# Two more turns of u given to the DMA crossbar, and another search over the order of instructions

## The chip, the cores and the metric

One core of one Trainium2 chip. The metric is the device time of one execution in microseconds (us); the profile's span is some 2 us shorter than the time of the same execution. Each kernel was run several times (an execution over 1.5% above the fastest of its kernel counts as slow).

## The reference

Attention with a block-causal mask over 8 batches, then a mixer over tokens and over channels:

```
scores = q @ k.T / 8                    # 8 batches, 8 heads, 576 tokens, 64 wide
attn   = softmax(where(block_i >= block_j, scores, -1e9))      # blocks of 64 tokens
x  = (attn @ v) as [batch, 576, 512]
h  = relu(x.T @ w_tok1) @ w_tok2        # over tokens, 576 -> 256 -> 576
u  = x + h.T
h2 = relu(u @ w_ch1) @ w_ch2            # over channels, 512 -> 1536 -> 512
out = u + h2                            # float32
```

## The kernel before

The kernel keeps everything in bfloat16 on the chip. Its parts are operations in a planner, which knows a cost for each, simulates the engines with a list schedule, perturbs priorities at random, keeps what ends earlier, and emits the instructions in the order found. The order is therefore fixed before the run, and a wait that the planner did not foresee stalls an engine on the spot (9.9 us of TensorE in the changed kernel).

The up projection over channels needs u transposed (`uT`, channels on partitions), the residual at the end needs u itself. Three ways occur:

```python
# batch 0: uT is made directly; at the down projection TensorE turns it back into the same bank
for m in range(NDM) if turned and part == 0 else ():
    nc.tensor.matmul(out=ps[:, 128*m : 128*(m+1)], lhsT=uT[b % 2][:, si, m, :], rhs=ident,
                     start=(m == 0), stop=False)
# batch 1: u is made, and TensorE transposes it (4 chunks, and one of leftover rows, umt)
for m in range(NDM):
    nc.tensor.transpose(ps[:, 128*m : 128*(m+1)], src[:, 128*m : 128*(m+1)], ident)
# batches 2 to 7: the DMA crossbar transposes it, 256 KB at a time, issued from SP
nc.sync.dma_start_transpose(out=uT[b % 2][:, 2*f : 2*f+2]..., in_=ut[:, 2*f : 2*f+2, :]...)
```

All loads of q, k, v and of the weights after the first are issued by GpSimd and cast float32 to bfloat16 on the way. q and k have a ring of three buffers, v of two, so batch b's loads run while earlier batches compute. The down projection's weights come in three parts:

```python
for c in range(0, NDC, 4):
    nc.gpsimd.dma_start(out=wc2_sb[:, c : c + 4, :],
        in_=moe_w_ch2[128*c : 128*(c+4), :].rearrange("(p c) t -> p c t", c=4))
```

How the planner counts transfers: it has one clock for GpSimd's queue (`soft`) and one for SP's and ScalarE's (`hard`). A load is counted after earlier transfers of SP, but a transfer of SP is never delayed by loads:

```python
if e == "POOL": soft = max(soft, hard, first) + o.xfer
else:           hard = max(hard, first) + o.xfer
```

The softmax here doesn't subtract the row's maximum and nothing guards it: scores larger than these inputs give would overflow.

Of the kernel before, what the change touches and what calls it, by code (L numbers as in the profile page):

```python
# [30 lines left out]
class Plan:  # L31
# [37 lines left out]
    def search(self, tries):  # L69

        prios = [o.prio for o in self.ops]
        modes = [o.mode for o in self.ops]
        slots = {name: list(free) for name, free in self.free.items()}

        def run(prios):
            for o, prio, mode in zip(self.ops, prios, modes):
                o.prio, o.mode = prio, mode
            self.free = {name: list(free) for name, free in slots.items()}
            try:
                order = self.run()  # L80
            except ValueError:
                return math.inf, ()
            return max(o.end for o in order if not o.quick), order

        rnd = random.Random(0)
        movable = [n for n, prio in enumerate(prios) if abs(prio) < 4e3]
        best = run(prios)[0]
        for _ in range(tries):
            moved = list(prios)
            count, width = rnd.choice((1, 2, 4, 8, 30, 100)), rnd.choice((0.3, 1, 3, 10))  # L90
            for n in rnd.sample(movable, count):
                moved[n] += rnd.uniform(-width, width)
            end = run(moved)[0]
            if end <= best:
                best, prios = end, moved
        return run(prios)[1]
# [98 lines left out]
def kernel(  # L195
# [71 lines left out]
    def bank_of(note):  # L267
        return mm[note["slot"]]
# [486 lines left out]

    def first_uT(x_done, a_done, w2_ready):

        xt, at = x_sb[0], aT[0]
        done = []
        for m in range(NDM):  # L760
            bank = {}

            def emit(o, m=m, bank=bank):
                for c in range(4):
                    nc.tensor.matmul(  # L765
                        out=bank_of(bank)[:, 128 * c : 128 * c + 128],
                        lhsT=xt[:, c, 128 * m : 128 * (m + 1)],
                        rhs=ident,
                        start=(c == 0),
                        stop=False,  # L770
                    )

            first = P.add(
                "PE", mm_cost(128, 4), emit, x_done[2 * m : 2 * m + 2] + pads["ident"], -2700 + m,
                take=[(BANK, bank)], urgent=1,
            )

            def emit(o, m=m, bank=bank):
                for t in range(NDT):
                    nc.tensor.matmul(  # L780
                        out=bank_of(bank),
                        lhsT=at[:, t, 128 * m : 128 * (m + 1)],
                        rhs=w2_sb[:, t, 0:512],
                        start=False,
                        stop=(t == NDT - 1),
                    )

            op = P.add("PE", mm_cost(512, 2), emit, [a_done[m], first] + w2_ready, -2700 + m, urgent=1)
            reads(("a", 0), op)
            reads(("x", 0), op)  # L790

            def emit(o, m=m, bank=bank):
                ps = bank_of(bank).rearrange("p (c s) -> p c s", c=4)
                if o.engine == "ACT":
                    nc.scalar.copy(uT[0][:, :, m, :], ps)
                else:
                    nc.vector.tensor_copy(uT[0][:, :, m, :], ps)

            done.append(P.add(EVAC, evac_cost(512), emit, [op], -2700 + m, give=[bank], urgent=1))
        return done  # L800

    def token_mix(b, x_done, w1_ready, w2_ready):
# [10 lines left out]
        if b == 0:  # L813
            a_all = [
                token_up(0, slice(128 * m, 128 * m + 128), (0, 1), x_done[2 * m : 2 * m + 2], [], w1_ready, -2800 + m, 1)
                for m in range(NDM)
            ]
            done = first_uT(x_done, a_all, w2_ready)
            prio = 0.5
        else:  # L820
            a_all = [
                token_up(b, slice(0, DM), (tt,), x_done, a_war, w1_ready, prio) for tt in range(NDT)
            ]
        for si in range(4 if b == 0 else 0, 4):
            bank = {}

            def emit(o, si=si, bank=bank):
# [54 lines left out]
                reads(("x", (b - 1 + i) % 3), um_rows[-1])  # L882


        crossbar = b >= 2
        for f in range(2 if crossbar else 0):
            def emit(o, f=f):
                nc.sync.dma_start_transpose(
                    out=uT[b % 2][:, 2 * f : 2 * f + 2].rearrange("p c m s -> p (c m) s"),
# [3 lines left out]
            op = P.add("SP", 2.0, emit, u_done[2 * f : 2 * f + 2] + uT_war, prio, xfer=3.0)  # L893
            reads(("u", b % 3), op)
            done.append(op)
        if crossbar and odd:
            def emit(o):
                nc.sync.dma_start_transpose(out=umT[pair % 2], in_=umt)

            op = P.add("SP", 1.0, emit, um_rows + reuse(("umT", pair % 2)), prio, xfer=1.0)  # L900
            reads(("um", pair % 2), op)
            um_done.append(op)
        for si in () if crossbar or b == 0 else range(4 + odd):
            bank = {}

            def emit(o, si=si, bank=bank):
                ps = bank_of(bank).bitcast(BF16)[:, 0:512]
                src = ut[:, si, :] if si < 4 else umt
                for m in range(NDM):
                    nc.tensor.transpose(  # L910
                        ps[:, 128 * m : 128 * (m + 1)], src[:, 128 * m : 128 * (m + 1)], ident
                    )

            deps = ([u_done[si]] if si < 4 else um_rows) + pads["ident"]
            deps += uT_war if si < 4 else reuse(("umT", pair % 2))
            op = P.add(
                "PE", mm_cost(128, 4), emit, deps, prio + 2 + 0.1 * si, take=[(BANK, bank)]
            )
            reads(("u", b % 3) if si < 4 else ("um", pair % 2), op)

            def emit(o, si=si, bank=bank):
                ps = bank_of(bank).bitcast(BF16)[:, 0:512].rearrange("p (m s) -> p m s", m=NDM)
                dst = uT[b % 2][:, si] if si < 4 else umT[pair % 2]
                if o.engine == "ACT":
                    nc.scalar.copy(dst, ps)
                else:
                    nc.vector.tensor_copy(dst, ps)

            op = P.add(
                EVAC, {"ACT": act_cost(512), "DVE": dve_cost(512, 2)}, emit, [op], prio, give=[bank]  # L930
            )
            (done if si < 4 else um_done).append(op)
        return done, um_done, u_done, um_rows

    a_even = {}
# [61 lines left out]
    def channel_down(b, g_done, wc2_ready, u_done, prio, mixed=False):  # L997
        chunks = [None] if mixed else list(range(4))
        gt = gmT[b // 2 % 2] if mixed else gT[b % 2]
        ut = um_sb[b // 2 % 2] if mixed else u_sb[b % 3]  # L1000

        turned = b == 0 and not mixed
        prev = None
        for n, si in enumerate(chunks):
            c0 = 0 if mixed else 128 * si
# [8 lines left out]
            for cols in (slice(0, 256), slice(256, 512)) if last else (slice(0, 512),):  # L1014
# [4 lines left out]
                for part in range(3):  # L1019
                    def emit(o, part=part, si=si, c0=c0, cols=cols, width=width, bank=bank):  # L1020
                        ps = bank_of(bank)[:, 0:width]
                        for m in range(NDM) if turned and part == 0 else ():
                            nc.tensor.matmul(  # L1023
                                out=ps[:, 128 * m : 128 * (m + 1)],
                                lhsT=uT[b % 2][:, si, m, :],
                                rhs=ident,
                                start=(m == 0),
                                stop=False,
                            )
                        for cc in range(4 * part, 4 * part + 4):  # L1030
                            nc.tensor.matmul(  # L1031
                                out=ps,
                                lhsT=gt[:, cc, c0 : c0 + 128],
                                rhs=wc2_sb[:, cc, cols],
                                start=(cc == 0 and not turned),
                                stop=(cc == NDC - 1),
                            )


                    gs = g_done[part : part + 1] if mixed else g_done[4 * part : 4 * part + 4]  # L1040
                    deps = [prev] + gs + wc2_ready[part : part + 1] + (u_done if part == 0 else [])
                    cost = mm_cost(width, 4) + (mm_cost(128, 4) if turned and part == 0 else 0)
                    prev = P.add(
                        "PE", cost, emit, deps, prio + 0.1 * n - 0.01 * part + cols.start * 1e-4,
                        take=[(BANK, bank)] if part == 0 else (),
                    )
                reads(("gm", b // 2 % 2) if mixed else ("g", b % 2), prev)
                if turned:
                    reads(("uT", b % 2), prev)

                def emit(o, si=si, oi=oi, n=n, cols=cols, width=width, bank=bank):
                    dst, ps = o_sb[oi][:, n % 2, cols], bank_of(bank)[:, 0:width]
                    if turned:
                        cast(o, dst, ps)
                    else:
                        nc.vector.tensor_tensor(  # L1056
                            out=dst, in0=ps, in1=(ut if mixed else ut[:, si, :])[:, cols], op=ADD
                        )

                op = P.add(  # L1060
                    EVAC if turned else "DVE", evac_cost(width), emit, [prev] + u_done + o_war, prio, give=[bank]
                )
                reads(("um", b // 2 % 2) if mixed else ("u", b % 3), op)
                halves.append(op)
# [55 lines left out]
                channel_down(p, g_done, wc2_ready, u_done, 10 * p + 4)  # L1120

    with tc.manual_schedule():
        for op in P.search(1000):
            op.emit(op)


# [28 lines left out]
```

## Time and profile before

| | kernel before |
|---|---|
| time, median | 306.5 us (306.05 to 306.92) |
| span of the profile | 304.3 us |
| TensorE busy | 98% |
| DMA before 68 us | about 200 GB/s; the load queue's packets take 130% of the 16 engines' time |
| crossbar transposes | 12 to `uT`, 3 to `umT`, all from 84.8 us on, land in 2.4 to 4.9 us |

A share over 100%, as this 130%, means that several packets are open on an engine at once. The lines themselves are in the prediction.

### The profile page before, as it was taken

To read this page: it belongs to the slowest core of one execution; us is meant where nothing else is said; L and a number is where in the kernel's file an instruction comes from. 1 tells how busy PE (TensorE), PEld (TensorE's weight loads), DVE (VectorE), ACT (ScalarE), POOL (GpSimd) and SP (SyncE) were. 2 spreads that over 40 slices of the span, in tenths; PEclk is the share of its full clock that TensorE was granted. 3 is DMA by queue.
4 is the path that set the end of the run, shared out by engine and by line. 5 is a ranking of instruction groups with operands and counts; after the bars stand their busy time and mean duration, and the time that the engine had idled before them with its cause. 6 is when DMAs were issued, how large, how long until landed. Compare 5 with 4: busy or idle time off the path is not lost.

```text
span 304.3 us, 7056 instructions
## 1 busy us (share of the span) xinstructions
PE 296.9 (98%) x2999; PEld 160.7 (53%) x3034; DVE 155.5 (51%) x380; ACT 164.6 (54%) x233; POOL 62.1 (20%) x96
## 2 busy tenths in 40 slices
PE   8999999999999999999999999999999999999995
PEld 4575456465454564555554564645446545555443
DVE  5566539989595599584987253615023021010112
ACT  5887855677855756875557856324413503615300
POOL 9766454702610602600140000000000000000000
PEclk9999999999999999999999999999999999999999
DMA  8999999995982998975193002033113222100133
GB/s 202 179 196 209 200 191 187 220 216 91 142 121 44 161 119 139 189 46 60 54 107 88 2 2 53 18 95 97 36 32 140 46 80 49 43 26 2 69 138 106
DMA packets 64383, 31.94 MB, mean 105 GB/s; under 512 B 53088, under 2 KB 55008, under 8 KB 64352
## 3 DMA queue, kind: packets, MB, share of 16 engines
q0 software_dynamic: 44320, 17.34, 48.9%
q1 hardware_dynamic: 19744, 13.57, 17.1%
q10 hardware_dynamic: 288, 0.59, 0.5%
q8 instruction: 23, 0.38, 0.5%
q14 instruction: 8, 0.07, 0.1%
HBM read 35.85 MB, written 9.44 MB: 149 GB/s over the span
## 4 chain that ended last, share of the span: by engine, by line
PE 95%; DMA 2%; issue 1%; DVE 1%; ACT 0%; ACTq 0%
PE mm L1031 31%; PE mm L947 28%; PE mm L555 10%; PE sc L508 10%; PE mm L736 6%; PE mm L829 4%; PE mm L974 4%; DMA gT<-in_q_dram 2%; PE mm L860 1%; PE mm L332 1%; PE mm L780 0%; PE mm L910 0%; DVE qT L393 0%; PE mm L1023 0%; PE mm L765 0%
## 5 line engine op out<-in xcount | busy, mean ns | idle before, releaser
L527 ACT ACTIVATE e_sb<-sc 128x1024 bf16<-128x1024 f32 x95 | 92.5, 1028 | 26.3 <-PE sc L508 24.5
L947 PE MATMUL mm<-uT,wc_sb 128*128 128x512 bf16 x384 | 91.2, 380 | 0.1
L1031 PE MATMUL mm<-wc_sb,gT 128*128 128x512 bf16 (+1 forms) x372 | 89.4, 372 | 1.5 <-issue 0.5
L722 ACT ACTIVATE gT<-mm 128x512 bf16<-128x512 f32 x74 | 44.2, 597 | 63.1 <-PE mm L947 62.8
L947 PEld LDWEIGHTS <-wc_sb 128*128 128x128 bf16 x384 | 41.9, 114 | 39.3 <-issue 3.9
L1031 PEld LDWEIGHTS <-gT 128*128 128x128 bf16 x396 | 36.9, 98 | 40.8 <-issue 3.3
L1056 DVE TENSOR_TENSOR o_sb<-mm,u_sb 128x512 f32<-128x512 f32 (+1 forms) x29 | 19.5, 672 | 74.5 <-PE mm L1031 74.3
L422 POOL DMA_DIRECT2D v<-in_v_dram x45 | 37.2, 839 | 35.3 <-PE sc L508 23.6
L508 PE MATMUL sc<-qT,kT 32*128 32x64 bf16 (+4 forms) x744 | 35.4, 281 | 0.5 <-DVE qT L393 0.5
L555 PEld LDWEIGHTS <-e_sb 128*128 128x128 bf16 x896 | 31.1, 97 | 8.0 <-issue 3.6
L555 PE MATMUL mm<-v,e_sb 128*128 128x65 bf16 x896 | 33.9, 193 | 0.1
L583 DVE TENSOR_TENSOR x_sb<-mm,rinv 128x320 bf16<-128x320 f32 x64 | 31.0, 491 | 2.0
L724 DVE TENSOR_SCALAR gT<-mm 128x512 bf16<-128x512 f32 x22 | 15.2, 689 | 15.9 <-PE mm L947 15.7
L844 DVE TENSOR_TENSOR u_sb<-mm,x_sb 128x512 bf16<-128x512 f32 x28 | 18.0, 686 | 10.2 <-PE mm L829 9.0
L393 DVE STREAM_TRANSPOSE qT<-qraw 128x288 int32<-128x288 int32 x32 | 21.6, 706 | 3.0 <-PE sc L508 2.1
L393 DVE STREAM_TRANSPOSE kT<-kraw 128x288 int32<-128x288 int32 x32 | 20.9, 703 | 4.3 <-DMA kraw<-in_k_dram 1.7
L508 PEld LDWEIGHTS <-kT 32*128 32x128 bf16 x752 | 12.3, 93 | 19.8 <-issue 16.7
L736 PE MATMUL mm<-x_sb,w_sb 128*128 128x512 bf16 (+1 forms) x98 | 18.0, 314 | 0.3
L533 DVE MEMSET e_sb<- 64x128 uint32 (+1 forms) x72 | 10.5, 153 | 14.7 <-ACT e_sb L527 11.4
L373 POOL DMA_DIRECT2D qraw<-in_q_dram x15 | 8.3, 552 | 42.2 <-DVE qT L393 28.5
L577 DVE RECIPROCAL rinv<-mm 128x5 f32<-128x5 f32 x64 | 11.4, 185 | 7.4 <-PE mm L555 6.7
L722 ACT ACTIVATE aT<-mm 128x512 bf16<-128x512 f32 (+1 forms) x15 | 8.1, 543 | 12.3 <-PE mm L736 12.3
(66 smaller groups left out, 175.6 us busy)
## 6 DMA issues: line engine op xcount, KB each, us to landing
out_dram<-o_sb SPq DMA_DIRECT2D x15, 512.0 KB, 2.9
kraw<-in_k_dram POOLq DMA_DIRECT2D x15, 288.0 KB, 7.7
qraw<-in_q_dram POOLq DMA_DIRECT2D x15, 288.0 KB, 7.2
v<-in_v_dram POOLq DMA_DIRECT2D x28, 128.0 KB, 6.9
wc_sb<-in_moe_w_ch_dram POOLq DMA_DIRECT2D x8, 192.0 KB, 7.1
wc_sb<-in_moe_w_ch_dram POOLq DMA_DIRECT2D x3, 512.0 KB, 10.4
out_dram<-o_sb SPq DMA_DIRECT2D x10, 128.0 KB, 2.3
v<-in_v_dram POOLq DMA_DIRECT2D x15, 64.0 KB, 6.1
```

The source lines that it names most:

```text
L393: nc.vector.transpose(dst[:, 0:S, :] .rearrange("p s e -> p (s e)") .bitcast(I32) .rearrange("p (a k) -> p k a", k=NB)[:, k0:k1], raw2.bit ...
L422: nc.gpsimd.dma_start(out=dst, in_=src)
L508: nc.tensor.matmul(out=home(n)[:, c0 : c0 + w], lhsT=kT[i][r, j0 : j0 + 128, par], rhs=qT[i][r, i0 : i0 + w, par], start=(par == 0), stop= ...
L527: nc.scalar.activation(dst, sc[SC.index(note["pool"])][:, :, 0:n], EXP, scale=scale)
L555: nc.tensor.matmul(out=u[:, I, 0:65], lhsT=w, rhs=vt[:, J, head, 0:65], start=(J == 0), stop=(J == I),)
L583: nc.vector.tensor_tensor(out=xt[:, :, 64 * head : 64 * head + 64], in0=u[:, :, 0:64], in1=ri.to_broadcast([128, 5, 64]), op=MULT,)
L722: nc.scalar.activation(dst, src, RELU)
L736: nc.tensor.matmul(out=bank_of(bank)[:, w * n : w * n + w], lhsT=wt[:, tt : tt + 255 : 2], rhs=xt[:, c, cols], start=(c == 0), stop=(c == 4),)
L844: nc.vector.tensor_tensor(out=ut[:, si, :], in0=bank_of(bank), in1=xt[:, si, :], op=ADD)
L947: nc.tensor.matmul(out=bank_of(bank), lhsT=wc1_sb[:, m, channels(cc)], rhs=uT[b % 2][:, :, m, :], start=(m == 0), stop=(m == NDM - 1),)
L1031: nc.tensor.matmul(out=ps, lhsT=gt[:, cc, c0 : c0 + 128], rhs=wc2_sb[:, cc, cols], start=(cc == 0 and not turned), stop=(cc == NDC - 1),)
L1056: nc.vector.tensor_tensor(out=dst, in0=ps, in1=(ut if mixed else ut[:, si, :])[:, cols], op=ADD)
```

## The change

The intent is to take 36 matmuls of 128 columns from TensorE, the engine that bounds the kernel (98% busy, 95% of the chain that ended last). Batch 0's u now comes from two crossbar transposes of `uT`, and batch 1's `uT` and `umT` from three of u. The planner gets another seed and 1,500 tries. The diff, cut to its core:

```diff
-        rnd = random.Random(0)
+        rnd = random.Random(3)
 ...
             done = first_uT(x_done, a_all, w2_ready)
+            for f in range(2):
+                def emit(o, f=f):
+                    nc.sync.dma_start_transpose(
+                        out=ut[:, 2 * f : 2 * f + 2, :].rearrange("p c (m d) -> p (c m) d", m=NDM),
+                        in_=uT[0][:, 2 * f : 2 * f + 2].rearrange("p c m s -> p (c m s)"),
+                    )
+                op = P.add("SP", 2.0, emit, done, 3.0 + 0.1 * f, xfer=3.0)
 ...
-        crossbar = b >= 2
-        for f in range(2 if crossbar else 0):
+        for f in range(2 if b else 0):
 ...   (TensorE's transposes of batch 1 and their evictions go)
-                        for m in range(NDM) if turned and part == 0 else ():
-                            nc.tensor.matmul(... lhsT=uT[b % 2][:, si, m, :], rhs=ident ...)
 ...   (the batch's eviction on either engine becomes VectorE's add of u)
-        for op in P.search(1000):
+        for op in P.search(1500):
```

More of the change, by code (lines that the diff above doesn't have):

```diff
@@ L818, in token_mix @@
             done = first_uT(x_done, a_all, w2_ready)
+            for f in range(2):
[5 more added lines that the diff above has]
+                op = P.add("SP", 2.0, emit, done, 3.0 + 0.1 * f, xfer=3.0)
+                reads(("uT", 0), op)
+                u_done.append(op)
             prio = 0.5
@@ L823, in token_mix @@
             ]
-        for si in range(4 if b == 0 else 0, 4):
+        for si in () if b == 0 else range(4):
             bank = {}
@@ L895, in token_mix @@
             done.append(op)
-        if crossbar and odd:
+        if odd:
             def emit(o):
@@ L902, in token_mix @@
             um_done.append(op)
-        for si in () if crossbar or b == 0 else range(4 + odd):
-            bank = {}
-            def emit(o, si=si, bank=bank):
-                ps = bank_of(bank).bitcast(BF16)[:, 0:512]
-                src = ut[:, si, :] if si < 4 else umt
-                for m in range(NDM):
-                    nc.tensor.transpose(
-                        ps[:, 128 * m : 128 * (m + 1)], src[:, 128 * m : 128 * (m + 1)], ident
-                    )
-            deps = ([u_done[si]] if si < 4 else um_rows) + pads["ident"]
-            deps += uT_war if si < 4 else reuse(("umT", pair % 2))
-            op = P.add(
-                "PE", mm_cost(128, 4), emit, deps, prio + 2 + 0.1 * si, take=[(BANK, bank)]
-            )
-            reads(("u", b % 3) if si < 4 else ("um", pair % 2), op)
-            def emit(o, si=si, bank=bank):
-                ps = bank_of(bank).bitcast(BF16)[:, 0:512].rearrange("p (m s) -> p m s", m=NDM)
-                dst = uT[b % 2][:, si] if si < 4 else umT[pair % 2]
-                if o.engine == "ACT":
-                    nc.scalar.copy(dst, ps)
-                else:
-                    nc.vector.tensor_copy(dst, ps)
-            op = P.add(
-                EVAC, {"ACT": act_cost(512), "DVE": dve_cost(512, 2)}, emit, [op], prio, give=[bank]
-            )
-            (done if si < 4 else um_done).append(op)
         return done, um_done, u_done, um_rows
@@ L1000, in channel_down @@
         ut = um_sb[b // 2 % 2] if mixed else u_sb[b % 3]
-        turned = b == 0 and not mixed
         prev = None
@@ L1021, in emit @@
                         ps = bank_of(bank)[:, 0:width]
-                        for m in range(NDM) if turned and part == 0 else ():
-                            nc.tensor.matmul(
-                                out=ps[:, 128 * m : 128 * (m + 1)],
-                                lhsT=uT[b % 2][:, si, m, :],
-                                rhs=ident,
-                                start=(m == 0),
-                                stop=False,
-                            )
                         for cc in range(4 * part, 4 * part + 4):
@@ L1034, in emit @@
                                 rhs=wc2_sb[:, cc, cols],
-                                start=(cc == 0 and not turned),
+                                start=(cc == 0),
                                 stop=(cc == NDC - 1),
@@ L1041, in channel_down @@
                     deps = [prev] + gs + wc2_ready[part : part + 1] + (u_done if part == 0 else [])
-                    cost = mm_cost(width, 4) + (mm_cost(128, 4) if turned and part == 0 else 0)
                     prev = P.add(
-                        "PE", cost, emit, deps, prio + 0.1 * n - 0.01 * part + cols.start * 1e-4,
+                        "PE", mm_cost(width, 4), emit, deps, prio + 0.1 * n - 0.01 * part + cols.start * 1e-4,
                         take=[(BANK, bank)] if part == 0 else (),
@@ L1047, in channel_down @@
                 reads(("gm", b // 2 % 2) if mixed else ("g", b % 2), prev)
-                if turned:
-                    reads(("uT", b % 2), prev)
                 def emit(o, si=si, oi=oi, n=n, cols=cols, width=width, bank=bank):
                     dst, ps = o_sb[oi][:, n % 2, cols], bank_of(bank)[:, 0:width]
-                    if turned:
-                        cast(o, dst, ps)
-                    else:
-                        nc.vector.tensor_tensor(
-                            out=dst, in0=ps, in1=(ut if mixed else ut[:, si, :])[:, cols], op=ADD
-                        )
+                    nc.vector.tensor_tensor(out=dst, in0=ps, in1=(ut if mixed else ut[:, si, :])[:, cols], op=ADD)
                 op = P.add(
-                    EVAC if turned else "DVE", evac_cost(width), emit, [prev] + u_done + o_war, prio, give=[bank]
+                    "DVE", dve_cost(width), emit, [prev] + u_done + o_war, prio, give=[bank]
                 )
```

## The prediction

> **What bounds the kernel now.** I read the page first (busy shares, slices, the chain that ended last), then the chain of work cut to the stretch that the change touches, then the DMA view of the same stretch, then groups by form.
>
> ```profile
> span 304.3 us, 7056 instructions
> ...
> PE 296.9 (98%) x2999; PEld 160.7 (53%) x3034; DVE 155.5 (51%) x380; ACT 164.6 (54%) x233; POOL 62.1 (20%) x96
> ...
> PE   8999999999999999999999999999999999999995
> ...
> DMA  8999999995982998975193002033113222100133
> ...
> PE 95%; DMA 2%; issue 1%; DVE 1%; ACT 0%; ACTq 0%
> ```
>
> TensorE is busy from the second slice to the last but one, and 95% of the chain that ended last is its own matmuls following each other. No other engine is above 54%. [...] I checked its waits from 20 us on: only 0.5 us of idle matmul time is named. The kernel is bound by the number of slots in TensorE's stream; what leaves that stream shortens the span, if nothing new waits. The DMA row is the second thing to note: it is near full from the start to about 68 us (nine slices of 7.6 us), and just there the change adds transfers.
>
> The chain of work from 38 to 68 us (start, length, what):
>
> ```profile
> by line: PE mm L1031 34.7%; PE mm L555 18.8%; PE sc L508 14.0%; PE mm L947 7.6%; PE mm L736 7.2%; PE mm L829 5.4%; PE mm L910 4.6%; PE mm L1023 3.0%; PE mm L974 3.0%; PE mm L860 1.8%; issue 1.1%
> ...
> 39.79 0.22 PE mm L1023 x4
> ...
> 40.88 0.22 PE mm L1023 x4
> ...
> 48.58 0.22 PE mm L1023 x4
> ...
> 52.14 0.23 PE mm L1023 x4
> ...
> 59.81 0.39 PE mm L910 x4
> ...
> 61.06 0.22 PE mm L910 x4
> ...
> 61.85 0.55 PE mm L910 x8
> ...
> 63.70 0.89 PE mm L974 x16
> 64.59 0.22 PE mm L910 x4
> ```
>
> Both removed groups lie on the chain: L1023 turns batch 0's u back, L910 transposes batch 1's u and the leftover rows. Their matmul records say 219 ns each, but that includes the pipeline; the chain gives the slot: 0.22 us for four, and L974, of the same width, has 0.89 us for 16, so 55 to 56 ns.
>
> Now the DMA, first over the stretch from 20 to 70 us, then the same kinds over the whole execution:
>
> ```profile
> q0 software_dynamic: 17449, 8.85, 130.5%
> ...
> out_dram<-o_sb SPq DMA_DIRECT2D x2, 512.0 KB, 7.3
> ```
>
> ```profile
> out_dram<-o_sb SPq DMA_DIRECT2D x15, 512.0 KB, 2.9
> ...
> uT<-u_sb SPq DMA_TRANSPOSE x12, 3.2
> ...
> umT<-um_sb SPq DMA_TRANSPOSE x3, 3.2
> ```
>
> In the crowded stretch one queue alone claims 130% of the 16 engines' time, and an output of 512 KB needs 7.3 us to land instead of 2.9. All existing crossbar transposes start at 84.8 us or later, where they land in 3.1 to 4.9 us. The new ones go where the DMA is full.
>
> [...]
>
> **The change part by part.**
> 1. Batch 0's turning back is removed: 4 chunks x 4 matmuls of 128 columns, on the chain 0.22 + 0.22 + 0.22 + 0.23 = 0.89 us. In its place two crossbar transposes write u from uT, and VectorE adds u where before a plain copy emptied the bank (two copies on ScalarE at 586 ns, two on VectorE at 691 ns; now four adds on VectorE at about 690 ns).
> 2. Batch 1's TensorE transposes are removed: 5 x 4 matmuls, on the chain 0.39 + 0.22 + 0.55 + 0.22 = 1.38 us. Twenty slots at 55 ns are 1.10 us; [...]. Five evictions go (three on VectorE at 422 ns, two on ScalarE at 586 ns); two transposes of 256 KB and one of 128 KB come in.
> 3. Sum on TensorE: 0.89 + 1.38 = 2.27 us, 0.7% of the time; 36 slots at 55 ns alone are 1.98 us.
> 4. ScalarE loses 2 x 0.586 + 2 x 0.586 = 2.3 us. VectorE loses 3 x 0.42 + 2 x 0.69 = 2.65 us and gains 4 x 0.69 = 2.76 us: no change in sum, although it is 9.4 of 10 us busy between 50 and 60 us. Neither sets the end.
> 5. SP issues five more transposes of 1.2 to 2.2 us each, 6 to 11 us, on a queue that has two outputs before 84 us. No cost.
> 6. DMA: 4 x 256 + 128 KB is 1.15 MB, at the 200 GB/s that this stretch moves about 5.8 us more of full DMA before 70 us (an estimate from those two numbers). Loads land later by up to that.
> 7. The search takes another seed and 1,500 tries instead of 1,000, so the order of everything may move, also where the work is unchanged. A short visit to the scores between long matmuls costs about a quarter of a microsecond beyond its columns: 12 matmuls between two such visits take 2.71 us where 24 unbroken ones take 5.18, so 0.12 us to leave, and the visit itself has 0.56 us for 1,024 columns of four at a time, 0.43 us at the 0.216 us of an unbroken 512, so 0.13 us more. But a set of scores takes both score buffers, so two sets cannot easily run back to back, and the number of visits is nearly fixed. With 98% busy there is little left to find: I allow 0.2 us of gain, and 1.5 us either way of chance.
>
> Does the new latency come to the path? For batch 0, uT is complete at 27.0 us (last eviction on ScalarE) and u is first needed by the down projection at 39.8 us: 12.8 us of slack. With the 7.3/2.9 = 2.5 of the outputs applied to 3.2 us, a transpose lands in about 8 us (an estimate); two of them fit. For batch 1 the last u row is written at 63.6 us, the last copy of uT ends at 65.3 and is first read at 67.1 us. By crossbar it would be ready at about 63.6 + 1.3 + 8 = 73 us. That would be a stall of 6 us if the order stayed, but it does not: the planner counts 2.0 + 0.7 + 3.0 + 1.3 = 7.0 us for a first transpose and 10.0 us for the second, puts other TensorE work in between, and takes u earlier. For batches 2 to 7 it did exactly that (batch 2: transposes issued from 84.8 us on, other batches' work meanwhile) and no TensorE wait is named. Its 10 us for the last transpose of the pair covers my 8 plus issue.
>
> **The rivals.**
> - The full credit, 304.2 us: all 2.27 us leave the chain. For it: both groups on the chain, no idle. Against: the crowded DMA.
> - A new wait takes the place. Batch 1's up projection, or its leftover rows, waits for a late transpose, because the planner does not count the other queue's load against SP's transfers, and TensorE's order is fixed before the run. For: 130% queue share, 7.3 us outputs. Against: the planner's margin. It would give back 1 to 4 us: 305 to 308 us.
> - The new transfers delay loads. The third part of the down projection's weights is issued at 28.5 us and these parts take 9.5 to 11.8 us, so they land near 39 us, just before use at about 42.5 us; batch 0's transposes start at about 27 us, beside them. A delay of 3 us would be covered, one of 5.8 would cost 2 us: 306 us.
> - A lucky or unlucky order: the longer search saves as much again, 302 to 303 us, or finds an order that the chip runs worse, 306 us.
>
> **Range and chances.** From the median of 306.5 us: minus 2.3 for the slots, minus 0.2 for the search, plus 0.3 as my weight for the two DMA rivals (about one chance in six of 2 us), makes 304.3 us. The range is 302.6 to 306.3 us: below, a search gain of 1.7 us on top; above, nearly everything given back. Faster by over 2% needs less than 300.4 us, that is 6.1 us, nearly three times what leaves TensorE: 3%. Slower by over 2% needs over 312.6 us, a stall much above any that I found: 2%. Within 2%: 95%.
>
> **What the changed profile would show.** L1023's and L910's counterparts are gone and TensorE has 36 matmuls fewer, with 1.5 to 2.3 us less in the chain. The chain stays at about 95% TensorE. There are 16 transposes to uT and u in place of 12, and four to umT; the early ones land in 5 to 9 us. No DMA is named as releaser of a TensorE wait beyond some tenths of a microsecond between 26 and 75 us. I am wrong if the up projection of batch 1 or the down projection of batch 0 sits behind a transpose for over 1 us, if a weight load waits for the weights of the down projection, or if the chain after 90 us, where the work is the same, differs by over 1 us: then the order of the search, not the crossbar, made the time.

## The result, and the profile after

The changed kernel took 323.5 us, median of four executions: 320.55, 322.66 and 324.31 us, and 329.65 us, which counts as slow; the median of the three fast ones is 322.7 us. The ratio to before is 1.0523 (95% interval 1.0444 to 1.0601). Ratios here are the mean time of one kernel's fast runs over that of the other's of the same rounds, so not quite the ratio of the medians. The result is correct; the change is 5% slower, far outside the range.

From the page after:

```profile
span 320.9 us, 6985 instructions
...
PE 299.7 (93%) x2966; PEld 161.1 (50%) x3001; DVE 158.7 (49%) x386; ACT 158.7 (49%) x222; POOL 62.0 (19%) x96
...
PE   8999709997899999999999999999999999999994
...
PEclk9999966999799999999999999999999999999999
DMA  9999999999999179694094101512103331301205
GB/s 202 187 200 199 147 49 162 190 185 204 168 192 104 19 107 180 117 164 78 2 122 37 67 3 65 67 67 49 67 0 67 131 65 33 133 0 42 91 0 165
...
PE 79%; DMA 15%; POOL 2%; DVE 1%; issue 1%; POOLq 0%
```

The chain that ended last was 95% TensorE and is 79%; 15% of it is DMA. The PE row has a hole in its sixth slice (40 to 48 us). In the same slice the DMA row stands at 9 and the DMA moves 49 GB/s: busy and slow at once. The clock row then shows 6: TensorE was idle from 37.9 us, and from 43.0 us it was granted half speed. A smaller dent stands near 80 us.

Who waited for whom (total, times, longest), TensorE's matmuls, after:

```profile
PE mm L1001 <- DMA wc_sb<-in_moe_w_ch_dram: 9.9, 1, 9.9
PE mm L954 <- DMA umT<-um_sb: 2.6, 1, 2.6
```

DMA issues, after, with KB and median us to landing:

```profile
wc_sb<-in_moe_w_ch_dram POOLq DMA_DIRECT2D x3, 512.0 KB, 23.0
...
u_sb<-uT SPq DMA_TRANSPOSE x2, 19.8
```

The first wait is the down projection's for its weights. They landed in 9.5 to 11.8 us before, and take 23.0 now (median; 20.9 to 24.1). The new order also issues them later, from 26.9 us on in place of 23.3. Batch 0's two transposes were issued at 27.1 and 28.5 us and landed 15.8 and 23.7 us later. The second wait is the mixed rows' up projection (the leftover rows of batches 0 and 1 together) for batch 1's transpose of the leftover rows, 8.2 us on its way.

The sum: 9.9 us of stall; then half clock, which the clock records give from 43.0 to 53.2 us, of which 47.8 to 53.2 was worked (eight matmuls of 512 columns took 3.11 us there, 0.39 us each, against 0.216 at full clock in the kernel before), so 2.7 us lost; then 2.6 us for `umT`, and half clock again to 83.95 us, from 81.2 worked, 1.4 us lost. That is 16.6 us, and the span grew by 16.6; that the two agree so well is partly luck, for the sum leaves out what the new order costs and what the empty slots save. The 2.3 us that I had credited are nowhere in it; the experiments say why.

### The profile page after: what moved, and what is told of

It is laid out like the page before. It is cut to its first block, busy times and chain, and to the rows that moved or that the text cites. A ratio compares the mean times of both kernels' runs of the same rounds, so it can differ in the third digit from the quotient of the medians.

```text
span 320.9 us, 6985 instructions
## 1 busy us (share of the span) xinstructions
PE 299.7 (93%) x2966; PEld 161.1 (50%) x3001; DVE 158.7 (49%) x386; ACT 158.7 (49%) x222; POOL 62.0 (19%) x96
## 4 chain that ended last, share of the span: by engine, by line
PE 79%; DMA 15%; POOL 2%; DVE 1%; issue 1%; POOLq 0%
PE mm L1001 28%; PE mm L927 24%; DMA wc_sb<-in_moe_w_ch_dram 9%; PE mm L555 7%; PE sc L508 7%; PE mm L736 5%; PE mm L954 4%; PE mm L840 3%; DMA umT<-um_sb 3%; DMA qraw<-in_q_dram 2%; DMA w_sb<-in_moe_w_tok_dram 2%; POOL v L422 1%; PE mm L871 1%; DVE um_sb L888 0%; DVE o_sb L1020 0%
## 5 line engine op out<-in xcount | busy, mean ns | idle before, releaser
L1001 PE MATMUL mm<-wc_sb,gT 128*128 128x512 bf16 (+1 forms) x376 | 89.3, 374 | 11.8 <-DMA wc_sb<-in_moe_w_ch_dram 9.9
L722 ACT ACTIVATE gT<-mm 128x512 bf16<-128x512 f32 x69 | 41.2, 597 | 63.4 <-PE mm L927 63.2
L1020 DVE TENSOR_TENSOR o_sb<-mm,u_sb 128x512 f32<-128x512 f32 (+1 forms) x33 | 22.3, 675 | 71.9 <-PE mm L1001 71.5
L724 DVE TENSOR_SCALAR gT<-mm 128x512 bf16<-128x512 f32 x27 | 18.6, 689 | 29.8 <-PE mm L927 29.2
L736 PE MATMUL mm<-x_sb,w_sb 128*128 128x512 bf16 (+1 forms) x98 | 17.9, 314 | 0.4
L533 DVE MEMSET e_sb<- 64x128 uint32 (+1 forms) x72 | 10.5, 153 | 14.2 <-ACT e_sb L527 11.0
L954 PE MATMUL mm<-umT,wc_sb 128*128 128x128 bf16 x192 | 13.7, 231 | 2.6 <-DMA umT<-um_sb 2.6
L722 ACT ACTIVATE gmT<-mm 128x512 bf16<-128x512 f32 x10 | 6.0, 597 | 19.3 <-PE mm L954 19.3
```

The costliest lines, as they stand in the source:

```text
L722: nc.scalar.activation(dst, src, RELU)
L736: nc.tensor.matmul(out=bank_of(bank)[:, w * n : w * n + w], lhsT=wt[:, tt : tt + 255 : 2], rhs=xt[:, c, cols], start=(c == 0), stop=(c == 4),)
L954: nc.tensor.matmul(out=bank_of(bank)[:, 128 * c : 128 * (c + 1)], lhsT=wc1_sb[:, m, channels(cc)], rhs=umT[pair % 2][:, m, :], start=(m == 0),
L1001: nc.tensor.matmul(out=ps, lhsT=gt[:, cc, c0 : c0 + 128], rhs=wc2_sb[:, cc, cols], start=(cc == 0), stop=(cc == NDC - 1),)
L1020: nc.vector.tensor_tensor(out=dst, in0=ps, in1=(ut if mixed else ut[:, si, :])[:, cols], op=ADD)
```

## The experiments

Batch 0's part is taken first. In the first four kernels and in the kernel with smaller weight loads the planner's input is the changed kernel's, so that the order of instructions on TensorE is the same to the last one; only what is emitted differs.

**Batch 0's transposes taken out** (wrong result).

```diff
-                    nc.sync.dma_start_transpose(out=ut[...], in_=uT[0][...])
+                    nc.vector.memset(ut[:, 2 * f : 2 * f + 2, :], 0.0)
```

> The changed kernel with its order of instructions unchanged on TensorE, ScalarE and GpSimd; only batch 0's two crossbar transposes are taken out, VectorE fills u with zeros instead (wrong result on purpose). Theory A, the transposes collide with the loads in flight at 27 us: the stall of 9.9 us for the down projection's weights at 38 to 48 us and the half clock after it go, together some 12 us, so 309 to 313 us, and the third part of these weights lands in about 10 us in place of 23. Theory B, the new order of the search is bad in itself (loads asked for too late): the stall stays and the time is 319 us or more.

310.8 us, ratio 1.0141 (1.0104 to 1.0178). The wait for the weights is gone, and these parts land in 10.6 us (median). Batch 0's two transposes, in this very order, cost some 12 us (11.9 between the medians of the fast executions). The wait for `umT` is still there with 3.5 us.

**Batch 1's transposes taken out as well** (wrong result; zeros in their place).

> As drop0, and batch 1's three transposes taken out too (zeros by VectorE, wrong result on purpose). What is left is the change's gain on TensorE with this order and without any new transfer. Theory A: 303 to 307 us, that is, within 1 us of my predicted 304.3 or somewhat above, as zeros cost VectorE about 2 us. Theory B: over 315 us.

307.6 us, ratio 1.0034 (1.002 to 1.0049): another 3.2 us gone, no TensorE wait for a DMA left, clock full to the end (1.000 in the mean), as in the kernel before. The time is a little above the 303 to 307 us that I wrote for theory A, but theory B, that the order as such makes the 17 us, falls. The kernel is 1 us slower than before, although TensorE has 36 matmuls fewer and no transfer came in. One wait of TensorE is as long as that:

```profile
PE mm L555 <- DVE e_sb L533: 1.0, 1, 1.0
```

It ends at 73.8 us. VectorE had then been busy almost without pause since 58.5 us, 1.2 us of it with the zeros in place of batch 1's transposes. So this microsecond is probably made by the experiment itself, and batch 1's collision may be worth some 4 us.

**Plain copies in place of batch 0's transposes** (wrong result): the same bytes on the same queue, first in rows of 2 KB, then in pieces of 256 bytes.

```diff
+                    nc.sync.dma_start(out=ut[...]"p (c d)", in_=uT[0][...]"p (c m s)")     # copy0
+                    for e in range(2):                                                      # copy0_256
+                        nc.sync.dma_start(out=to[:, e], in_=of[:, 4 * e : 4 * e + 4])       # 4 pieces of 256 B per row
```

> The changed kernel, same order; batch 0's two transposes are plain copies of the same bytes on the same queue, one row of 2 KB for each partition (wrong result on purpose). Theory A1, it is the crossbar's way of moving [...]: copies land in under 8 us, and the time is that of drop0 within 2 us, 309 to 313. Theory A2, it is the 0.5 MB more on a full DMA, whatever their form: still 318 us or more.

> As copy0, but the plain copies are cut into pieces of 256 bytes, as many packets of that size as the transposes have (2,048), in four transfers. Tells the packet size from the transposing. [...] these copies are slow to land (over 12 us), [...] and the time is within 3 us of copy0. If small packets alone hold up the loads as the transposes did: 318 us or more, with the weights landing in about 23 us.

311.7 us, ratio 1.0175 (1.014 to 1.0209), and 313.8 us, ratio 1.0235 (1.0213 to 1.0256). The copies landed in 9.2 us (I had said under 8) and 11.6 us (I had said over 12), the weights in 13.3 and 12.3 us (medians), TensorE's wait for them was 0.2 us and nothing. So neither the bytes nor the size of the pieces does it: half a megabyte of copies costs about 1 us over drop0, cut small about 3. What makes the 12 us is transposing.

Below is the DMA view from 36 to 46 us for three kernels: GB/s in 40 slices, then queue, packets, MB and share of 16 engines; q0 are the loads, q1 is SP's queue. First the changed kernel:

```profile
GB/s 134 147 127 109 80 135 83 34 45 8 140 158 156 163 148 140 63 69 30 16 16 17 43 46 19 43 37 25 18 40 42 23 24 22 124 147 167 158 75 52
...
q1 hardware_dynamic: 1706, 0.43, 107.5%
q0 software_dynamic: 1696, 0.35, 73.7%
```

With copies of 256 bytes:

```profile
q0 software_dynamic: 2487, 1.40, 97.8%
q1 hardware_dynamic: 1837, 0.45, 34.9%
```

And with no transfer in their place (drop0):

```profile
q0 software_dynamic: 3506, 1.96, 139.4%
```

In the same 10 us the loads move 1.96 MB alone, 1.40 MB beside 0.45 MB of small copies, and 0.35 MB beside 0.43 MB of transposes. The copies' packets took a third of the engines' time, the transposes' as many packets took three times that.

The packets' own records say more. Worked out from them (packets per us, median and mean ns of one):

```
                              256 B of SP         loads, 128 B        loads, 4 KB
copies,     31 to 36 us        55 (31, 30)        131 (32, 31)         42 (322, 323)
transposes, 31 to 36 us        58 (31, 62)         47 (32, 54)         40 (322, 327)
copies,     37 to 41 us       365 (31, 30)        386 (31, 31)        4.2 (322, 322)
transposes, 36 to 40 us       247 (31, 55)        243 (31, 45)        4.5 (322, 327)
transposes, 41 to 44 us        49 (321, 359)       46 (291, 183)      3.0 (322, 322)
transposes alone, before,
            86 to 89 us       683 (18, 21)          -                   -
```

With 40 to 42 packets of 4 KB per us beside them (first two rows), copies and transposes alike get through some 55 small packets per us (55 and 58). It did not last: from 31 to 36 us both kernels moved under 300 of their 2,048 small packets, and the copies landed in 11.6 us. So this stretch does not tell transposes from copies.

When 4 KB packets have become few (4.2 and 4.5 per us), both speed up, the copies to 365 packets per us and the transposes to 247 (rows three and four). Then the two part: the transposes fall back. From 41 to 44 us, 3.0 packets of 4 KB per us go with 49 transpose packets and 46 load packets in all, and 31 GB/s, and a transpose packet takes 321 ns (median) in place of 31 (from 44 to 46 us it was 225 transpose packets per us again). Why they fall back is not shown. That the few large packets alone do it, two records speak against: from 39 to 40 us 358 transpose packets went beside the same 3 large ones, and in the kernel gate1 below transposes took 13.3 and 19.5 us with no packet of 4 KB beside them.

**Smaller packets in the weights' load**, correct result: four loads, each with 1 KB per partition, in place of one with 4 KB.

```diff
+                for i in range(4):
+                    nc.gpsimd.dma_start(out=wc2_sb[:, c + i, :], in_=moe_w_ch2[...][:, i])
```

> The changed kernel, same order (four DMA issues on GpSimd for each of three), with the down projection's weights loaded in rows of 1 KB as written and not of 4 KB. Theory C, [...]: with 1 KB packets [...] the transposes land in under 12 us in place of 16 and 24, the stall of 9.9 us shrinks to under 4, and the time is 310 to 317 us. Theory D, any load beside a transpose is as bad, whatever its packets: 319 us or more.

318.7 us, ratio 1.0407 (1.038 to 1.0434). Transposes now run at 182 packets per us beside 77 packets of 1 KB per us, three times the 58 beside 4 KB ones; they land in 12.3 and 15.3 us, and TensorE waits 2.4 us for the weights in place of 9.9. So the size of the load's packets matters, as theory C has it, but the miss is plain as well: landing and time lie outside what I wrote for C, and the time just under what I wrote for D. Half clock still lasted from 39.9 to 46.8 us and from 74.1 to 77.5 us, and `umT`, which the weights do not touch, was late by 2.6 us.

**The search alone, and the change with the search of before.**

> The kernel before with the change's search alone (other seed, 1,500 tries in place of 1,000), no transpose moved. My prediction allowed a gain of 0.2 us and 1.5 us either way: 305 to 308 us. That the changed kernel without its new transposes still took 307.6 us, though 36 matmuls had left TensorE, makes me expect the upper half, 306.5 to 308. A theory that the search by itself costs several per cent would have 315 us or more.

> All the change's transposes, with the search of before (old seed, 1,000 tries). If the collision of the crossbar with the loads is general, and not a mishap of one order: again 315 to 330 us, with a transposed u of batch 0 landing in over 12 us and a TensorE wait of several us for a DMA. If the order of the changed kernel was the mishap: 304 to 308 us.

The search alone: 308.3 us, ratio 1.0061 (1.0044 to 1.0079), slightly above what I wrote. The planner's own count of the end was 304.4 us for the kernel before and 304.7 for this one; more tries from another seed had not found anything better even by its own count. The transposes with the old search: 330.7 us, ratio 1.0739 (1.0683 to 1.0795), TensorE waiting 13.9 us for v and 5.1 for `umT` (330.4 us without the slow one of its four executions; just above what I wrote). Another order, another victim, the same collision (batch 0's transposes landed in 17.9 us, median, the weights in 25.9). For it the planner counted 303.7 us, and 302.6 for the changed kernel.

**Batch 1 alone by the crossbar**, batch 0 turned back on TensorE.

```diff
-        crossbar = b >= 2
+        crossbar = b >= 1
```

> Batch 0 turned back on TensorE as before, batch 1 by the crossbar, with the change's search. 20 of the 36 matmuls gone. If batch 1's transposes, too, meet the loads (until about 70 us): a wait of TensorE for the transposed leftover rows of 2 to 4 us, 307 to 312 us. If only batch 0's transposes meet the weights: 304.5 to 306 us.

313.2 us, ratio 1.0204 (1.0174 to 1.0234), a little above the range. The transposes were issued at 60.8 to 64.3 us beside loads of q, k and v and landed in 8.8, 9.8 and 11.0 us; TensorE waited 4.8 us for `umT`. The collision does not need the down projection's weights.

**Keeping loads and transposes apart.** GpSimd, which issues the loads, reads an element of each transposed tile before it issues the loads of batch 3.

```diff
+            if p == 1:
+                def hold(o):
+                    for n, t in enumerate((uT[1][:, 0, 0], uT[1][:, 2, 0], umT[0][:, 0])):
+                        nc.gpsimd.tensor_copy(landed[:, n : n + 1], t[:, 0:1])
+                gate = [P.add("POOL", 0.4, hold, uT_done + um_done, -1e3)]   # batch 3's loads depend on it
```

> As b1_only (batch 0 turned back on TensorE, batch 1 by the crossbar, the change's search), but batch 3's loads wait on GpSimd until batch 1's three transposes have landed, so that fewer loads are in flight beside them. If the collision with the loads is what costs: the three transposes land in under 6 us, TensorE waits under 1 us for the leftover rows, and the time is 305 to 308 us, against 313.2 for b1_only. If the transposes are late for another reason: 311 us or more.

> The order of gate1 on every engine, without GpSimd's wait for the transposes: the loads are as free as their buffers let them. The pair tells the gate from the order. If the wait is what keeps them apart: the transposes land later than in gate1 by over 2 us and the time is 2 to 6 us longer. If the order alone does it: the same within 1 us.

> gate1 with the old seed and 1,000 tries: the spread that the search brings to the same work. The planner's own count is 305.7 us against 303.9 for gate1, so if it counts rightly 2 us more than gate1, 306 to 310 us; and again no transpose beside loads that lands in over 8 us.

With the gate, 313.5 us, the mean of the four fast executions of six, ratio 1.0219 (1.0185 to 1.0253); the same order without the wait, 319.7 us, the mean of the two fast ones of four, ratio 1.0421 (1.0358 to 1.0485). With the wait batch 1's transposes landed in 2.5, 4.0 and 4.5 us, without it in 7.6, 7.8 and 8.6 us. That is the pair that I wanted, and yet gate1 missed its 305 to 308 us. The reason stands in its waits and in the landings between 75 and 100 us, which are batch 2's transposes:

```profile
PE mm L948 <- DMA uT<-u_sb: 3.4, 1, 3.4
```

```profile
DMA to landing us min/median/max: 13.3/16.4/19.5
```

The same two without the wait:

```profile
PE mm L948 <- DMA uT<-u_sb: 6.1, 1, 6.1
```

```profile
DMA to landing us min/median/max: 16.0/18.6/21.2
```

I first took it that the loads which the gate had held back met batch 2's transposes, and wrote so in the expectation of gate_all_s0 below. The pair speaks against that: without the wait batch 3's loads went out at 54 to 60 us, 14 us earlier, and batch 2's transposes landed later still. What they met in both kernels are loads issued between 78 and 90 us, with packets of 2,304 and 128 bytes, which this order puts there; in the order of b1_only batch 2's transposes landed in 3.1 and 3.3 us. Part of the 6 us between the pair lies here too, at batch 2. With the old seed the gate gives 307.6 us, ratio 1.0025 (1.0007 to 1.0044); batch 2's transposes took 9.1 and 11.2 us there too (over the 8 us that I allowed), but nothing waited for them.

**The kernel before with a longer search only.**

> The kernel before with seed 7 and 4,000 tries, no other change; of eight seeds the planner counts it lowest, 303.9 us against 304.4 for the kernel before and 304.7 for search_only, which took 308.3. If the planner's count carries over to the chip: 305.5 to 306.3 us, a little below before. If differences of half a microsecond in its count mean nothing on the chip: anywhere in 305.5 to 309.

Six executions fall into two groups: 307.8 to 308.0 us, and 313.1 to 314.1 us, which count as slow. The ratio of the fast ones is 1.0036 (1.0017 to 1.0054). The planner's 303.9 did not carry over. The profile fell into the slow group; its clock was at half speed from 12.8 to 26.5 us, which I have not followed up.

**What was still open.** First, what the 36 slots are worth in one and the same order. Second, whether keeping all loads and transposes apart removes the loss. The first kernel is the one before in its own order, with the 36 matmuls not issued (wrong result; the copies read u untransposed):

```diff
-                        for m in range(NDM) if turned and part == 0 else ():
+                        for m in ():
 ...
-                for m in range(NDM):
+                for m in ():
                     nc.tensor.transpose(
```

> The kernel before in its own order, only the 36 matmuls that the change removes not issued (batch 0's turning back, batch 1's transposes; the copies read u untransposed, wrong result on purpose), no new transfer. The step of my prediction that counts slots says 1.98 to 2.27 us less: 304.2 to 304.8 us against 306.5 to 306.8. If TensorE's slots were not what bounds here: no gain, 306 us or more.

305.5 us against 306.5, ratio 0.9972 (0.9947 to 0.9997): 0.9 us (0.1 to 1.6 by the interval), not 2.0 to 2.3. The profiled execution, 306.3 us, is one of the slower of six: matmul by matmul, its TensorE was 0.8 us behind the kernel before's already at 30 us, before the first slot that is empty, and level with it at 67 us. So it shows 0.7 us won. A wait that the kernel before does not have, and the chain from 38 to 68 us, by line:

```profile
PE mm L860 <- DVE u_sb L844: 0.8, 1, 0.8
```

```profile
by line: DMA kraw<-in_k_dram 75.4%; POOL v L422 7.4%; issue 7.3%; PE mm L555 6.4%; PE mm L1031 6.3%; PE sc L508 4.5%; PE mm L974 3.0%; PE mm L947 2.9%; PE mm L829 2.9%; DVE qT L393 2.3%; PE mm L860 2.1%; DVE kT L393 2.0%; POOL qraw L373 1.9
...
30.36 12.19 DMA kraw<-in_k_dram
...
46.93 10.41 DMA kraw<-in_k_dram
```

The shares count a piece in full: of the first load's 12.19 us only 4.6 lie in the window. In the kernel before the same stretch was TensorE almost alone. At 52.4 us TensorE had won 1.1 us. Then VectorE, on its way to batch 1's u, waited for a load of k that landed at 57.3 us, and TensorE for VectorE. So in this execution the load took back part of what the empty slots had won. The same load landed at 55.4 us in the profile of the kernel before; whether it came later because of the empty slots or by chance, one profile does not tell. That a second bound lies close behind TensorE is suggested here, not shown.

The second question: the gate for every batch from 1 to 5, in two orders, and gate1 in the order that the planner counts lowest of all.

```diff
-            if p == 1:
+            if 1 <= p < 6:          # batch p+2's loads wait for batch p's transposes
```

> The gate of gate1 for every batch from 1 on: the loads of batch p+2 wait for batch p's transposes, so that the loads held back for batch 1 do not meet batch 2's transposes, as they did in gate1 (batch 2's landed in 13.3 and 19.5 us there). Seed 0, 2,000 tries. If collisions are the whole loss: every transpose lands in under 6 us, no TensorE wait for a transpose, 304.5 to 307.5 us. If the gate starves later batches: waits for q, k or v, 308 us or more.

> The same with seed 5, which the planner counts as 0.1 us better: 304.5 to 307.5 us; the difference from the other seed shows what the order alone does, up to 2 us by search_only.

> gate1 with seed 1 and 2,000 tries; the planner counts 303.0 us, the least of all orders with a gate (gate1 303.9, gate1_old 305.7). If the planner's count were to be trusted: the fastest of all, 304 to 306 us. If it leaves out the collisions and these decide: batch 2's transposes meet the loads again and it takes 308 us or more.

307.2 us, ratio 1.0019 (0.9991 to 1.0047); 307.1 us, ratio 1.0016 (0.999 to 1.0042); and 313.8 us, ratio 1.0249 (1.0209 to 1.0289). With the gates every transpose lands in time; in the second of them those to `uT`, all 14:

```profile
DMA to landing us min/median/max: 3.1/3.2/4.1
```

Those to `umT` take at most 4.6 us, and no TensorE wait for a transpose is left. In that profile GpSimd sat 23.2 and 13.8 us until batch 1's and batch 2's transposes had landed, so the waits do hold loads back; a twin of these two orders without them was not run. The third shows the planner's blindness: 303.0 us by its count, and in fact batch 2's transposes met the loads again (10.5 to 13.1 us) and TensorE waited 4.2 us for one. Kept apart in these two orders, the crossbar was harmless for batches 1 to 7 (307.2 and 307.1 us against 306.5), and it gained nothing: no version with a right result beats the kernel before. Batch 0's transposes were never run apart from the loads.

| kernel | time, us | what it tells |
|---|---|---|
| changed | 322.7 | median of the fast executions (323.5 with the slow one) |
| without batch 0's transposes | 310.8 | batch 0's collision: 11.9 us |
| without batch 1's either | 307.6 | batch 1's collision: 3.2 us or more |
| search alone | 308.3 | this seed's order: +1.8 us |
| before, 36 slots empty | 305.5 | the slots: -0.9 us |
| all loads kept apart (batch 0 on TensorE) | 307.1 | no collision, no gain |

The +1.8 us of the order and the -0.9 us of the slots add up to about the 1.0 us by which the kernel without any new transposes lies above before. Its order is not that of search_only, and it has a wait of 1.0 us behind its own zeros, so nothing should be read into that.

## Why the prediction was wrong

- *What bounds the kernel.* "What leaves that stream shortens the span, if nothing new waits" was right as far as it went, and the condition failed. It was also too sure: 98% busy did not say how close the next bound was. With the 36 slots empty and nothing new to wait for, the time fell by 0.9 us.
- *Part 3, the slots.* I know of no error in the count of 36 at 55 ns. The credit of 2.27 us was mis-sized: it was 0.9 us (0.1 to 1.6) in a fixed order, and in the one profile part of the rest went to a wait behind a load of k before 60 us.
- *Part 6 and the second and third rivals, the DMA.* This is the step that failed. I treated a crossbar transpose as 256 KB more on a full DMA: 5.8 us in all, and a landing of about 8 us from the outputs' slowdown of 2.5. For plain copies that was nearly right (9.2 us, and 1 us of time). Transposes took 15.8 and 23.7 us and brought the loads down with them: the weights took 23.0 us where I allowed for 5.8 us more. I had named these weights as the place of danger, and sized the harm at 2 us; it was 9.9 us of stall and 2.7 us of half clock, and the half clock was in none of my rivals. To a slowdown of over 2% I had given 2%. I also had less room than I wrote: in the profile before, the third part of the weights landed at 40.3 us, not near 39.
- *The evidence I had, and how I misread it.* I took the existing transposes (3.1 to 4.9 us from 84.8 us on) as proof that the planner's allowance works. Their packets show that in the kernel before those of batch 2 ran with no load packets beside them (86 to 89 us: 683 per us, and nothing else). They were no sample of what the change would do. I noted that "the new ones go where the DMA is full" and scaled by a factor taken from another kind of transfer.
- *The planner's margin.* Its 7 and 10 us did not cover 8 to 24. Its clock for SP's transfers ignores the loads; that the margin of 10 us "covers my 8" hung on my 8.
- *Part 7, the search.* I allowed 0.2 us of gain and 1.5 us either way; it lost 1.8 us, for a reason that I have not found. The loss is a little outside what I allowed, and the sign of the gain was wrong.
- *The signs that I named.* Two of the three that would prove me wrong appeared: a projection sat behind a transpose for over 1 us (2.6 us), and the weights for the down projection were waited for.

## What to carry to other kernels

Before moving work to a DMA path, look at whether its existing uses ran beside the same traffic, not only at how fast they landed; the landing time measured on a quiet DMA (3.1 to 3.3 us for 256 KB) said nothing here about a busy one (15.8 and 23.7 us). Crossbar transposes beside a stream of loads slowed both in these runs (the weights landed in 23.0 us in place of 10.6 without batch 0's transposes, medians), and most of the stall was for the loads (9.9 us in the changed kernel, against 2.6 us for a transpose): keep them apart in time with a real wait, at every transpose, for a wait at the first alone left the next one among later loads (13.3 and 19.5 us to land in gate1). And before crediting removed work, empty its slots in the unchanged order and time that: here it was worth some 0.4 of its count.
